# Attention and gated feed-forward on one core: own tiles for the copied sums, fewer exponential tiles, weight splits queued later

## The chip, the cores and the metric

One core of a Trainium2 chip runs the whole kernel in one launch. The metric is the device time of an execution in microseconds; three runs were taken, and the median is used. A profile of one further execution goes with them.

## What is computed

Input `x` has 2048 tokens of 512 features. All data are float32.

```
xn = layernorm(x)
q, k, v = split(xn @ wqkv)             # 32 heads of 16 features
s = concat_heads(softmax(q k^T / 4) v) @ wo
g = silu(((xn @ w_gate) * (xn @ w_up)) @ w_down)      # 1792 hidden features
out = x + s * g
```

## The kernel before

**Precision.** Products of weights and activations are made of three products of a fast float32 format: a value is split into a high part (a cast) and a low part (value minus high part), and high by high, high by low and low by high are added up. Weights are loaded in float32 into a "raw" tile and split by GpSimd, two instructions a tile: `split`, `split_raw`, `split_rows`. Scores carry the split in their contraction (48 rows: high, high, low against high, low, high), and the product of probabilities and V is in plain float32.

**Attention.** Heads go in 8 groups of 4, queries in 4 chunks of 512, so there are 32 units (`NU`), each of 16 rounds (`kt`, 128 keys each). In a round the main loop does, for each of the 4 heads `j`:
- `expo`: a matmul `t` of keys by queries into a PSUM bank of the pool `st` (3 banks), then the exponential by ScalarE into a tile `e` from `etile()`;
- `score`: a matmul `s` of queries by keys for the unit ahead (`LEAD` = 21 rounds ahead), and VectorE's maximum over it. Two more rows of the `t` matmul subtract that maximum;
- `step()`, which runs work that was put off by `soon(n, fn)` for n steps, and at some `j` (`GAPS`) a piece of filler.

At every even round `values()` runs the work in `before_values`, steps the finishing of heads, and calls `block(prev)`: 8 matmuls of the 8 `e` tiles of the two rounds before by V, in four column groups, into another bank of `st` named `pv`. ScalarE copies that bank. A unit's first block is copied into the tile `acc` (1 buffer); each later one goes into another `etile()`, and GpSimd adds it to `acc`. `etile()` has `EBUFS` = 12 buffers, shared by the exponentials, the copied sums and, at the start, raw weights of V.

**Heads.** `finish(i)` is a generator that `values()` steps: transpose `acc` into `tr` (VectorE), reciprocal of the row sums, multiply the heads into a tile `on` (GpSimd, or VectorE for the last four units), transpose `on` back into `tr`, and store it to DRAM (`OD`). For the last unit the heads stay on the chip and are split by `last_heads`.

**Filler.** The projections, the feed-forward part (`ffn`) and the output projection (`ending`) are generators whose matmuls are dealt out between the score matmuls by `Filler`, 6 gaps a cycle of two rounds, and a row of sums (`pair`) over two or three cycles. `pair` uses the lower and the upper 64 rows of TensorE at once. After its first half ScalarE reads one element (`look`), after its second `ffn` copies `g` on ScalarE, and VectorE multiplies `u` by `g` at the next `values()`. A row's last matmuls fall on gap 2 of an even round, so that the copy stands in ScalarE's program between the third and the fourth exponential of that round.

**Order.** The instructions of TensorE, ScalarE and VectorE keep the order in which the program gives them. GpSimd and the DMA queue of SyncE are put in order when the program is built, by a scheduler that takes what is ready by its own reckoning; only for the first 18 rounds is their order tied too. A tile that is used again waits for the last use of what was in it.

Of the kernel before, what the change touches and what calls it, by code (L numbers as in the profile page):

```python
# [11 lines left out]
F32 = mybir.dt.float32  # L12
# [7 lines left out]
P = 128  # L20
# [13 lines left out]
GAPS = [(0, 1, 2), (1, 2, 3)]  # L34
SLOTS = 24 * (NC * (NG // 2 - 1) + 1) + 36 * NF * NC
SPLIT_ROUNDS = 4
EBUFS = 12
HBUFS = 2
QBUFS = 2
FINAL_AT = 8  # L40
# [9 lines left out]
def body(ctx, tc, x, wqkv, wo, wg, wu, wd, out):  # L50
# [53 lines left out]
        pool.memset(V[:, tts, H * VW:], 1.0)  # L104

    ones_columns(slice(0, 8))
    on = keep.tile([P, 16, 32], F32, name="on")
    pool.memset(on, 0.0)

    fst = {}  # L110

# [36 lines left out]
    def etile():  # L148
        return ep.tile([P, 512], F32, name="e", bufs=EBUFS)

    qkv = ExitStack()
    qp = qkv.enter_context(tc.tile_pool(name="qkv", bufs=1))
    xh, xl = [[(qp if c else keep).tile([P, ND, 512], F32R, name=f"{n}{c}" if c else f"f{n[1]}") for c in range(NC)]
# [5 lines left out]
    def split(name, src):  # L159

        raw = wtile(name + "r")
        dma(raw, src.rearrange("(d p) f -> p d f", p=P))
        return split_raw(name, raw)

    def split_raw(name, raw, after=None):
        hi, lo = [wtile(name + n) for n in "hl"]
        cast = pool.tensor_copy(hi, raw)
        if after is not None:
            tc.add_manual_dep(cast.ins, after.ins.name, BEHIND, reason="keeps the port free for the layer norm")
        pool.tensor_tensor(lo, raw, hi, op=OP.subtract)  # L170
        return hi, lo
# [184 lines left out]
    def gu_weights(f):  # L356
        fs = slice(f * P, (f + 1) * P)
        return [split(n, w[:, fs]) for n, w in (("w1", wg), ("w0", wu))]

    def ffn(nxt):  # L360
        fp = fst["fp"]
        for c in range(NC):
            if c == 0:
                fh, fl = xh[0], xl[0]
            else:
                fh, fl = [keep.tile([P, ND, 512], F32R, name=n) for n in ("fh", "fl")]
                dmar(fh, XD[c][0])
                dmar(fl, XD[c][1])
            y = fp.tile([P, 4, D], F32, name="y")
            for ti, fs in enumerate(THIRDS):  # L370
                hh = fp.tile([P, 5, 512], F32R, name="hh")
                hl = fp.tile([P, 5, 512], F32R, name="hl")
                dh = fp.tile([P, 5, D], F32R, name="dh")
                dl = fp.tile([P, 5, D], F32R, name="dl")
                for i, f in enumerate(fs):
                    ws = nxt
                    if not (c == NC - 1 and f == NF - 1):
                        nxt = gu_weights((f + 1) % NF)
                    outs = []
                    yield from pair(outs, [("misc", f"{n}{c}_{f}") for n in "gu"], [terms(lambda d: wh[:, d], lambda d: wl[:, d],  # L380
                                                 lambda d: fh[:, d], lambda d: fl[:, d], ND) for wh, wl in ws])
                    g = fp.tile([P, 512], F32, name="g", bufs=1)
                    nc.scalar.activation(g, outs[0], AF.Copy)
                    h = fp.tile([P, 512], F32, name="h", bufs=1)
                    before_values.append(lambda h=h, u=outs[1], g=g, hi=hh[:, i], lo=hl[:, i]: product(h, u, g, hi, lo))
                    raw = fp.tile([P, D], F32, name="wdr", bufs=2)
                    dma(raw, wd[f * P:(f + 1) * P])
                    pool.tensor_copy(dh[:, i], raw)
                    pool.tensor_tensor(dl[:, i], raw, dh[:, i], op=OP.subtract)
                if c == NC - 1 and fs[-1] == NF - 1:  # L390
                    fst["y"] = y
                    fst["w"] = [keep.tile([P, ND, D], F32R, name=n) for n in ("fh", "fl")]
                    for d in range(ND):
                        raw = fp.tile([P, D], F32, name="wdr", bufs=2)
                        dma(raw, wo[d * P:(d + 1) * P])
                        split_rows(raw, *[t[:, d] for t in fst["w"]])
                for t in range(0, 4, 2):
                    outs = []
                    yield from pair(outs, [("misc", f"y{c}_{ti}_{u}") for u in (t, t + 1)], [terms(lambda i: hh[:, i, u * P:(u + 1) * P],
                                                 lambda i: hl[:, i, u * P:(u + 1) * P],  # L400
                                                 lambda i: dh[:, i], lambda i: dl[:, i], len(fs)) for u in (t, t + 1)])
                    for n, o in enumerate(outs):
                        def add(o=o, y=y[:, t + n], first=ti == 0, n=n):
                            if first and n:
                                nc.vector.tensor_copy(y, o)
                            elif first:
                                nc.scalar.activation(y, o, AF.Copy)
                            else:
                                nc.vector.tensor_tensor(y, o, y, op=OP.add)
                        before_values.append(add)  # L410
            later.append(silu(fp, c, y))
# [205 lines left out]
    def block(todo):  # L617

        i = todo[0][0]
        g = i // NC  # L620
        o = psum("st", f"pv{i}")
        for n, (_, kt, es) in enumerate(todo):
            for j in range(4):
                h0 = (4 * g + j) * VW
                nc.tensor.matmul(o[32 * j:32 * j + 32], V[:, kt, h0:h0 + 32], es[j],  # L625
                                 start=n == 0, stop=n == len(todo) - 1)
        if todo[0][1] == 0:
            sums[i] = keep.tile([P, 512], F32, name="acc", bufs=1)
            nc.scalar.activation(sums[i], o, AF.Copy)
        elif i == NU - 1 and kt >= NT - 2:  # L630
            nc.vector.tensor_tensor(sums[i], o, sums[i], op=OP.add)
        else:
            part = etile()
            nc.scalar.activation(part, o, AF.Copy)  # L634
            pool.tensor_tensor(sums[i], sums[i], part, op=OP.add)

    def finish(i):

        g, c = divmod(i, NC)
        tr = keep.tile([P, 16, 32], F32, name="tr", bufs=1)  # L640
        tn = tr.rearrange("p b e -> p (b e)")
        yield
        nc.vector.transpose(tn, sums.pop(i))
        rc = keep.tile([P, 16, 1], F32, name="rc", bufs=1)
        nc.vector.reciprocal(rc, tr[:, :, DH:DH + 1])
        late = i >= NU - NC
        (nc.vector if late else pool).tensor_tensor(on[:, :, 0:DH], tr[:, :, 0:DH], rc.to_broadcast([P, 16, DH]),
                                                         op=OP.mult)
        yield
        nc.vector.transpose(tn, on.rearrange("p b e -> p (b e)"))  # L650
        if i == NU - 1:
            fst["tn"] = tn
            return
        dma(OD[c][4 * g:4 * g + 4], tn)
        finished.add(i)


# [6 lines left out]
    def early():  # L664
# [5 lines left out]
        for which in (1, 0):  # L670
            wraw.append(wtile(f"w{which}r"))
            dma(wraw[-1], wqkv[:, which * D:which * D + P].rearrange("(d p) f -> p d f", p=P))
        norm["raws"] = raws = [etile() for _ in range(ND)]
        for d in range(ND):
            dma(raws[d], wqkv[d * P:(d + 1) * P, 2 * D:])
        for tt in range(4, NT):
# [7 lines left out]

        def warm(n):
            for _ in range(n):
                nc.tensor.matmul(psum("x", "warm"), ident, on.rearrange("p b e -> p (b e)"), start=True, stop=True)

        warm(6)
        first = (0, 1), (2, 3)  # L690
# [76 lines left out]
    def filler(wq0):  # L767
        yield from proj_pair(0, [(wq0, 0, 2), (wq0, 0, 3)])
        for m in range(1, NG // 2):
            wk, wq = fst.get(("qk", m)) or (qk_weights(m, 1), qk_weights(m, 0))  # L770
            for c in range(NC):
                yield from proj_pair(m, [(wk, 1, c), (wq, 0, c)])
                if m == 1 and c:
                    after = fst["high"].ins.name
                    for n, src in enumerate((xh, xl)):
                        put = sync.dma_start(XD[c][n].bitcast(F32), src[c].bitcast(F32))
                        tc.add_manual_dep(put.ins, after, BEHIND, reason="not before the first exponentials")
                if m == NG // 2 - 1 and c == NC - 2:
                    nxt = gu_weights(0)
        run_ahead()  # L780
        flush()
        qkv.close()
        fst["fp"] = ffp.enter_context(tc.tile_pool(name="ffn", bufs=1, reuse_waits="tile"))
        yield from ffn(nxt)
# [52 lines left out]
    prev = []  # L837

    def values():
        run_ahead()  # L840
        step_small(heads)
        block(prev)
        if prev[-1][1] == NT - 1:
            heads.append(finish(prev[0][0]))
            step_small(heads)
        prev.clear()
# [63 lines left out]
```

## Time and profile before

| | |
|---|---|
| median of 3 runs | 1803.99 us (1798.45 to 1805.04) |
| profiled execution | 1804.02 us, its span 1802.2 us |
| TensorE (PE) busy | 1758.0 us, 98% |
| VectorE (DVE) busy | 1447.8 us, 80% |
| ScalarE (ACT) busy | 1326.7 us, 74% |
| GpSimd (POOL) busy | 891.8 us, 49% |
| granted TensorE clock | 0.988 |

A row of the timeline reads: start and duration in us, engine, line, operation, tiles written and read, shape, count, and in brackets the engine's idle time before it and what ended it. A row of the waits reads: who waited, for whom, us in total, times, the longest. PEld is TensorE's loading of weights, which runs beside its matmuls. A matmul's end is modelled, so TensorE is read by the starts of its matmuls.

### The profile page before, as it was taken

What the parts mean: (1) busy time and instruction counts of PE and PEld (TensorE: products, weight loads), DVE (VectorE), ACT (ScalarE), POOL (GpSimd) and SP (SyncE); (2) the same over time, 40 slices, a digit from 0 to 9 for tenths busy, and PEclk for the clock granted to TensorE, in tenths of its full rate; (3) what the DMA queues carried; (4) which work ended last, traced back from release to release, by engine and by line L of the source; (5) the groups of instructions that cost most, each with busy time, mean ns of one, the idle gap of its engine ahead of it and who ended that gap; (6) DMA issues with size and microseconds to landing.
All of it is one profiled execution on the core that took longest, in us unless ns stands there. A gap on an engine that the chain in (4) does not pass through costs nothing.

```text
span 1802.2 us, 35104 instructions
## 1 busy us (share of the span) xinstructions
PE 1758.0 (98%) x13578; PEld 1064.8 (59%) x13578; DVE 1447.8 (80%) x2440; ACT 1326.7 (74%) x2576; POOL 891.8 (49%) x920
## 2 busy tenths in 40 slices
PE   9999999899999999999999999999999999998897
PEld 5656556565665666566556665566655566555544
DVE  6878888788888888888888888888878888887613
ACT  5357777677777778777777877777777777776663
POOL 4314554653644556365354755435466365355641
PEclk9999999999999999999999999999999999999989
DMA  5317524511231312321132211312233121111421
GB/s 199 115 57 229 199 99 127 141 41 44 63 69 52 97 50 66 71 69 48 38 84 84 80 49 57 75 40 63 80 77 82 29 68 51 40 46 47 157 86 70
DMA packets 117234, 145.78 MB, mean 81 GB/s; under 512 B 12620, under 2 KB 74060, under 8 KB 114380
## 3 DMA queue, kind: packets, MB, share of 16 engines
q1 hardware_dynamic: 117068, 143.55, 27.1%
q8 instruction: 106, 1.74, 0.4%
q14 instruction: 60, 0.49, 0.1%
HBM read 95.94 MB, written 47.45 MB: 80 GB/s over the span
## 4 chain that ended last, share of the span: by engine, by line
PE 86%; POOL 6%; DMA 2%; issue 2%; DVE 2%; ACT 2%; SPq 0%; POOLq 0%; ACTq 0%; DVEq 0%
PE pv L625 23%; PE t L612 17%; PE s L587 12%; PE g L275 5%; PE y L275 5%; PE g L279 4%; PE u L275 4%; PE y L279 4%; PE u L279 3%; PE p L275 2%; PE v L256 2%; PE p L279 1%; PE z L275 1%; POOL acc L64 1%; DVE mx L589 1%
## 5 line engine op out<-in xcount | busy, mean ns | idle before, releaser
L589 DVE TENSOR_REDUCE mx<-s 128x1 f32<-128x512 f32 x2048 | 1278.1, 684 | 260.1 <-PE s L587 181.4
L614 ACT ACTIVATE e<-t 128x512 f32<-128x512 f32 x2048 | 1117.7, 605 | 125.5 <-POOL acc L64 52.9
L612 PE MATMUL t<-qs,ks 50*128 50x512 f32 x2048 | 811.1, 417 | 28.0 <-ACT e L614 25.4
L587 PE MATMUL s<-ks,qs 48*128 48x512 f32 x2048 | 802.8, 422 | 2.6 <-DVE mx L589 2.5
L612 PEld LDWEIGHTS t<-qs,ks 50*128 50x128 f32 x2048 | 363.7, 187 | 330.3 <-ACT e L614 131.1
L64 POOL TENSOR_TENSOR acc<-acc,e 128x512 f32<-128x512 f32 x223 | 290.8, 1304 | 484.3 <-ACT e L634 481.7
L625 PE MATMUL pv<-e,V 128*32 128x512 f32 x4096 | 494.3, 600 | 0.0
L587 PEld LDWEIGHTS s<-ks,qs 48*128 48x128 f32 x2048 | 353.1, 186 | 35.4 <-DVE mx L589 6.4
L634 ACT ACTIVATE e<-pv 128x512 f32<-128x512 f32 x223 | 133.3, 598 | 229.8 <-PE pv L625 229.6
L625 PEld LDWEIGHTS pv<-e,V 128*32 128x32 f32 x4096 | 107.3, 109 | 239.7 <-issue 188.3
L64 POOL CAST w0h<-w0r 128x512 fp32r<-128x512 f32 x60 | 36.6, 611 | 135.5 <-PE u L275 64.0
L279 PE MATMUL g<-fh,w1h 64*128 64x512 f32 x224 | 91.0, 406 | 0.0
L279 PE MATMUL y<-dh,hh 64*128 64x512 f32 x224 | 90.3, 403 | 0.0
L275 PE MATMUL u<-fh,w0h 64*128 64x512 f32 x224 | 89.5, 400 | 0.0
L279 PE MATMUL u<-fh,w0h 64*128 64x512 f32 x224 | 89.0, 397 | 0.0
L275 PE MATMUL y<-dh,hh 64*128 64x512 f32 x224 | 88.8, 396 | 0.0
L279 PE MATMUL u<-fh,w0l 64*128 64x512 f32 x224 | 88.7, 396 | 0.0
L275 PE MATMUL y<-dl,hh 64*128 64x512 f32 x224 | 88.6, 396 | 0.0
L275 PE MATMUL g<-fh,w1h 64*128 64x512 f32 x224 | 88.5, 395 | 0.0
L275 PE MATMUL g<-fh,w1l 64*128 64x512 f32 x224 | 88.5, 395 | 0.0
L275 PE MATMUL u<-fl,w0h 64*128 64x512 f32 x224 | 88.4, 395 | 0.0
L279 PE MATMUL u<-fl,w0h 64*128 64x512 f32 x224 | 88.4, 395 | 0.0
(257 smaller groups left out, 3061.9 us busy)
## 6 DMA issues: line engine op xcount, KB each, us to landing
w1r<-in_wg_dram SPq DMA_DIRECT2D x56, 256.0 KB
w0r<-in_wu_dram SPq DMA_DIRECT2D x56, 256.0 KB
wdr<-in_wd_dram SPq DMA_DIRECT2D x56, 256.0 KB
qs<-QD SPq DMA_DIRECT2D x64, 192.0 KB
ks<-KD SPq DMA_DIRECT2D x12, 768.0 KB
KD<-hl SPq DMA_DIRECT2D x16, 512.0 KB
QD<-hl SPq DMA_DIRECT2D x16, 512.0 KB
OD<-tr SPq DMA_DIRECT2D x31, 256.0 KB
```

The source lines that it names most:

```text
L64: got = getattr(self.engine, name)(*args, **kw)
L256: nc.tensor.matmul(o, l(d), r(d), start=k == d == 0, stop=k == 2 and d == ND - 1)
L275: nc.tensor.matmul(outs[k], l[LOWER], r[LOWER], start=k == 0 and n == 0, stop=(stop or k == 0) and n == len(low) - 1, skip_group_check=k == 1)
L279: nc.tensor.matmul(outs[1 - k], l[UPPER], r[UPPER], start=k == 0 and m == 0, stop=(stop or k == 0) and m == len(high) - 1, skip_group_chec ...
L587: nc.tensor.matmul(o, QS[i][b:b + KB, pr, t * P:(t + 1) * P], k[b:b + KB, pr, kc * 512:(kc + 1) * 512], start=True, stop=True)
L589: nc.vector.tensor_reduce(MX[i][:, j, t, kc:kc + 1], o, axis=AX.X, op=OP.max)
L612: nc.tensor.matmul(o, k[b:b + KR, pr, kt * P:(kt + 1) * P], QS[i][b:b + KR, pr], start=True, stop=True)
L614: nc.scalar.activation(e, o, AF.Exp, scale=DH ** -0.5)
L625: nc.tensor.matmul(o[32 * j:32 * j + 32], V[:, kt, h0:h0 + 32], es[j], start=n == 0, stop=n == len(todo) - 1)
L634: nc.scalar.activation(part, o, AF.Copy)
```

## The change

- `EBUFS` goes from 12 to 10. The copied sums of blocks get two tiles of their own (`parts()`, `PBUFS` = 2), and so do two of the raw weights at the start.
- `acc` has 2 buffers. The zeroed tile `on` is gone; the warming matmuls at the start read a zeroed `acc` instead.
- `finish` multiplies the heads in place in `tr` and transposes them back into the unit's `acc`, which is stored. For the last two units it runs at once, without pauses, and VectorE adds the last block of unit 30 as it did for unit 31.
- `values()` steps the heads only where `before_values` is empty.
- `split` puts its two GpSimd instructions off by 6 steps. The load of `w_down` moves ahead of the pair `g`, `u`, and its split is put off by 8 steps. The projections' weights for the next group are asked for at chunk 2 of the group before.

```diff
-EBUFS = 12
+EBUFS = 10
+PBUFS = 2
...
-    on = keep.tile([P, 16, 32], F32, name="on")
-    pool.memset(on, 0.0)
+    idle = keep.tile([P, 512], F32, name="acc", bufs=2)
+    pool.memset(idle, 0.0)
...
+    def parts():
+        return ep.tile([P, 512], F32, name="part", bufs=PBUFS)
...
         raw = wtile(name + "r")
         dma(raw, src.rearrange("(d p) f -> p d f", p=P))
-        return split_raw(name, raw)
+        hl = [wtile(name + n) for n in "hl"]
+        soon(6, lambda: split_rows(raw, *hl))
+        return hl
...
                         nxt = gu_weights((f + 1) % NF)
+                    raw = fp.tile([P, D], F32, name="wdr", bufs=2)
+                    dma(raw, wd[f * P:(f + 1) * P])
+                    soon(8, lambda raw=raw, i=i, dh=dh, dl=dl: split_rows(raw, dh[:, i], dl[:, i]))
                     outs = []
...
-                    raw = fp.tile([P, D], F32, name="wdr", bufs=2)
-                    dma(raw, wd[f * P:(f + 1) * P])
-                    pool.tensor_copy(dh[:, i], raw)
-                    pool.tensor_tensor(dl[:, i], raw, dh[:, i], op=OP.subtract)
...
         if todo[0][1] == 0:
-            sums[i] = keep.tile([P, 512], F32, name="acc", bufs=1)
+            sums[i] = keep.tile([P, 512], F32, name="acc", bufs=2)
             nc.scalar.activation(sums[i], o, AF.Copy)
-        elif i == NU - 1 and kt >= NT - 2:
+        elif i >= NU - 2 and kt >= NT - 2:
             nc.vector.tensor_tensor(sums[i], o, sums[i], op=OP.add)
         else:
-            part = etile()
+            part = parts()
             nc.scalar.activation(part, o, AF.Copy)
             pool.tensor_tensor(sums[i], sums[i], part, op=OP.add)
...
         tr = keep.tile([P, 16, 32], F32, name="tr", bufs=1)
-        tn = tr.rearrange("p b e -> p (b e)")
-        yield
-        nc.vector.transpose(tn, sums.pop(i))
+        acc = sums.pop(i)
+        late = i >= NU - 2
+        if not late:
+            yield
+        nc.vector.transpose(tr.rearrange("p b e -> p (b e)"), acc)
         rc = keep.tile([P, 16, 1], F32, name="rc", bufs=1)
         nc.vector.reciprocal(rc, tr[:, :, DH:DH + 1])
-        late = i >= NU - NC
-        (nc.vector if late else pool).tensor_tensor(on[:, :, 0:DH], tr[:, :, 0:DH], rc.to_broadcast([P, 16, DH]),
-                                                         op=OP.mult)
-        yield
-        nc.vector.transpose(tn, on.rearrange("p b e -> p (b e)"))
+        (nc.vector if i >= NU - NC else pool).tensor_tensor(tr[:, :, 0:DH], tr[:, :, 0:DH],
+                                                            rc.to_broadcast([P, 16, DH]), op=OP.mult)
+        if not late:
+            yield
+        nc.vector.transpose(acc, tr.rearrange("p b e -> p (b e)"))
         if i == NU - 1:
-            fst["tn"] = tn
+            fst["tn"] = acc
             return
-        dma(OD[c][4 * g:4 * g + 4], tn)
+        dma(OD[c][4 * g:4 * g + 4], acc)
         finished.add(i)
...
-            wk, wq = fst.get(("qk", m)) or (qk_weights(m, 1), qk_weights(m, 0))
+            wk, wq = fst["qk", m]
             for c in range(NC):
+                if c == 2 and m + 1 < NG // 2:
+                    fst["qk", m + 1] = qk_weights(m + 1, 1), qk_weights(m + 1, 0)
                 yield from proj_pair(m, [(wk, 1, c), (wq, 0, c)])
...
     def values():
-        run_ahead()
-        step_small(heads)
+        if before_values:
+            run_ahead()
+        else:
+            step_small(heads)
         block(prev)
```

More of the change, by code (lines that the diff above doesn't have):

```diff
@@ L672, in early @@
             dma(wraw[-1], wqkv[:, which * D:which * D + P].rearrange("(d p) f -> p d f", p=P))
-        norm["raws"] = raws = [etile() for _ in range(ND)]
+        norm["raws"] = raws = [etile() if d < 2 else parts() for d in range(ND)]
         for d in range(ND):
@@ L686, in warm @@
             for _ in range(n):
-                nc.tensor.matmul(psum("x", "warm"), ident, on.rearrange("p b e -> p (b e)"), start=True, stop=True)
+                nc.tensor.matmul(psum("x", "warm"), ident, idle, start=True, stop=True)
         warm(6)
```

## The prediction

> **What bounds the kernel now.** I read the page's busy times first, then the timeline of ordinary rounds, the waits, and the timeline again where a wait is long.
>
> ```profile
> PE 1758.0 (98%) x13578; PEld 1064.8 (59%) x13578; DVE 1447.8 (80%) x2440; ACT 1326.7 (74%) x2576; POOL 891.8 (49%) x920
> ```
>
> TensorE is busy in 98% of the span; nothing else is near. So a change pays only by what it takes from, or adds to, TensorE's standing time. The attention loop gives TensorE one block of probability-times-V matmuls (L625) per two rounds. I call the time from one block's start to the next's a cycle, and count within it from the block's start, P. There are 256. One with a full load of filler (24 matmuls), after a `g` copy, and the start of the next:
>
> ```profile
> 1004.74 0.60 ACT L383 ACTIVATE g<-g 128x512 f32<-128x512 f32 x1
> 1004.87 1.92 PE L625 MATMUL pv<-e,V 128*32 128x512 f32 x16
> 1005.22 0.61 ACT L614 ACTIVATE e<-t 128x512 f32<-128x512 f32 x1
> 1006.72 0.50 PE L612 MATMUL t<-qs,ks 50*128 50x512 f32 x1
> 1006.86 0.60 ACT L634 ACTIVATE e<-pv 128x512 f32<-128x512 f32 x1 [0.52 <-PE pv L625]
> 1007.07 0.39 PE L612 MATMUL t<-qs,ks 50*128 50x512 f32 x1
> 1007.29 0.39 PE L275 MATMUL g<-fh,w1h 64*128 64x512 f32 x1
> 1007.75 0.39 PE L612 MATMUL t<-qs,ks 50*128 50x512 f32 x1
> 1011.60 1.93 PE L625 MATMUL pv<-e,V 128*32 128x512 f32 x16
> ```
>
> The cycle lasts 6.73 us. In it: the block to P+1.92; the first score matmul `t` at P+1.85, the second at P+2.20, the first filler at P+2.42, the third `t` at P+2.88. The third waits for the copy of the block's sums (P+1.99 to 2.59), since `st` has three PSUM banks. The second needs the bank that the fourth exponential of the round before the block empties. That one starts at P+0.35 and ends at P+0.96, with 1.2 us to spare. That spare time is what the change spends.
>
> Where is TensorE kept standing now? The waits:
>
> ```profile
> ACT e L614 <- POOL acc L64: 52.9, 36, 6.7
> PE t L612 <- ACT e L614: 25.4, 13, 5.0
> ACT acc L629 <- DVE tr L643: 9.2, 9, 2.1
> ```
>
> 36 times the fourth exponential waits for GpSimd's addition of the block before, because its `e` buffer was the one that held the block's copied sums. 13 times it is so late that TensorE itself stands. The first of these, the two largest, and between them a middling one with the next block's start:
>
> ```profile
> 192.30 0.50 PE L612 MATMUL t<-qs,ks 50*128 50x512 f32 x1 [0.58 <-ACT e L614]
> 331.51 1.92 PE L625 MATMUL pv<-e,V 128*32 128x512 f32 x16
> 337.31 0.60 ACT L614 ACTIVATE e<-t 128x512 f32<-128x512 f32 x1 [5.22 <-POOL acc L64]
> 337.96 0.79 PE L612 MATMUL t<-qs,ks 50*128 50x512 f32 x1 [4.10 <-ACT e L614]
> 344.83 1.92 PE L625 MATMUL pv<-e,V 128*32 128x512 f32 x16
> 347.19 0.60 ACT L614 ACTIVATE e<-t 128x512 f32<-128x512 f32 x1 [2.34 <-PE s L587]
> 347.84 0.49 PE L612 MATMUL t<-qs,ks 50*128 50x512 f32 x1 [0.67 <-ACT e L614]
> 348.18 0.40 PE L275 MATMUL u<-fh,w0h 64*128 64x512 f32 x1
> 352.48 1.92 PE L625 MATMUL pv<-e,V 128*32 128x512 f32 x16
> 1637.32 1.92 PE L625 MATMUL pv<-e,V 128*32 128x512 f32 x16
> 1644.70 0.79 PE L612 MATMUL t<-qs,ks 50*128 50x512 f32 x1 [5.03 <-ACT e L614]
> ```
>
> The middling one is my scale. The exponential ends at P+2.96, the second `t` issues 0.05 later, and the filler comes 0.34 behind it, not 0.22: a matmul that meets an idle TensorE costs 0.12 more. Late by 0.81 + 0.12 = 0.93; the cycle lasts 7.65 instead of 6.73, 0.92 longer. What is lost there comes back nowhere.
>
> **Part 1: ten `e` tiles instead of twelve (a loss).** A block reads the eight tiles of the two rounds before while the current round fills its own four: twelve. With ten, the third and fourth exponentials need the tiles that the block's first two matmuls read. In the built order they wait for those two, which now signal for themselves; before, only the block's last one did. When do they end?
>
> ```profile
> 1011.60 0.16 PEld L625 LDWEIGHTS pv<-e,V 128*32 128x32 f32 x8 [0.37 <-ACT e L614]
> 1012.06 0.13 PEld L625 LDWEIGHTS pv<-e,V 128*32 128x32 f32 x4 [0.30 <-issue]
> L625 PE MATMUL pv<-e,V 128*32 128x512 f32 x4096 | 494.3, 600 | 0.0
> ```
>
> The program's 8 matmuls run as 16, each in two halves, four at a time over four column groups. The later loads at P+0.46 mark the second four starting. If these are the second halves of the first four tiles, a tile is free at 0.46 + 0.60 = P+1.06; with the 0.07 that the copy shows behind the block's end, ScalarE starts at P+1.13. If both halves were among the first four, it would be P+0.69. One column group cannot take two halves at once, so I take 1.13. No later bound is open: each of the two signals by itself.
>
> The third exponential then runs from P+1.13. ScalarE takes its next work 0.48 later (1004.74 to 1005.22). The fourth runs from P+1.61 to 2.21, and the second `t` goes at P+2.26: 0.06 late, plus 0.12 for an idle TensorE: 0.18. But a `g` copy, or its like in the projections, stands in ScalarE's order between the two. Then the fourth runs from P+2.09 to 2.69, and `t` goes at 2.74: 0.54 + 0.12 = 0.66 late. How often?
>
> ```profile
> L383 ACT ACTIVATE g<-g 128x512 f32<-128x512 f32 x56 | 34.1, 609 | 0.0
> L312 ACT ACTIVATE qr<-p 128x512 f32<-128x512 f32 x13 | 8.0, 612 | 0.0
> L589 DVE TENSOR_REDUCE mx<-s 128x1 f32<-128x512 f32 x2048 | 1278.1, 684 | 260.1 <-PE s L587 181.4
> ```
>
> 69 cycles, each the first of its filler pair and full: 69 x 0.66 = 46 us. Of the other 174 up to 1691 us, 85 carry 18 or more filler matmuls and lose 0.18 to 0.23 (the tiny `look` read adds 0.05): 17 us. In 89, with 16 or fewer, the eight reductions of 684 ns pace TensorE, and 0.18 fits beside them: 0 to 2 us. Some 20 cycles have one more ScalarE copy behind the fourth exponential; it pushes the sums' copy past the third `t`, about 0.35 each: 7 us. Loss: 70 us, 17 by the earlier release (69 x 0.22, plus 2).
>
> **Part 2: own tiles for the copied sums (a gain).** Now the copy, not the exponential, waits for GpSimd, and for the addition two blocks back: about 12 us may pass instead of 5. The additions stand in GpSimd's built order where they stood, and the bursts of w_down splits are as long; I count nothing for the later queueing. The two largest stalls (13.32 - 6.73 = 6.6 us at 331.5; 7.6 at 1637.3) had additions late by less than that, and go. With a third of 4.0 and seven of 0.75 to 1.0 (the first is the `t` at 192.30 above, the last in the cycle at 1630): 24 us. Next in line is GpSimd's order for the hidden-layer splits, whose readers are a pair or more away.
>
> **Part 3: two tiles for a unit's sums, heads in place.** The copy that waited for the transpose no longer does. Six cycles were 0.46 to 0.77 longer by it: 3.4 us. Stepping the heads only where no other VectorE work is due takes perhaps half of 2.4 us of crowded cycles: 1. The in-place product and the transposes are as many and as large: 0.
>
> **Part 4: the end.** The heads of unit 30 finish four rounds sooner, so the output projection's third chunk moves into two cycles that had no filler, and its two pairs leave the tail.
>
> ```profile
> 1691.28 1.93 PE L625 MATMUL pv<-e,V 128*32 128x512 f32 x16
> 1742.50 1.92 PE L625 MATMUL pv<-e,V 128*32 128x512 f32 x16
> 1748.14 1.92 PE L625 MATMUL pv<-e,V 128*32 128x512 f32 x16
> 1768.17 1.93 PE L625 MATMUL pv<-e,V 128*32 128x512 f32 x16
> 1774.06 1.92 PE L625 MATMUL pv<-e,V 128*32 128x512 f32 x16
> 1778.09 1.93 PE L625 MATMUL pv<-e,V 128*32 128x512 f32 x16
> 1783.73 0.69 DVE L544 TENSOR_TENSOR h<-tr,g 128x512 fp32r<-128x512 f32 x1 [0.69 <-ACT g L543]
> 1796.62 0.40 PE L523 MATMUL z<-hl,h 128*128 128x512 f32 x1
> 1797.87 0.69 DVE L450 TENSOR_TENSOR y<-z,hh 128x512 f32<-128x512 f32 x1
> ```
>
> The twelve cycles from 1691.28 to 1778.09 take 86.8 us; three stand on late additions. In their place: one of 6.8, ten of 6.0 (1768.17 to 1774.06 is 5.89, plus 0.1 from part 1), one of 4.1: 70.9. I add 4 us: unit 31's row maxima still queue behind twelve GpSimd instructions, and VectorE's next output rows behind them, which held nothing up while TensorE stood anyway. 12 us gained. Then the last heads: their low halves are ready at 1784.42, and only the twelve last matmuls (0.23 each) and VectorE's six steps of 0.7 remain, to about 1789.6 instead of 1798.56: 9 us. Together 21.
>
> **Sum.** The profiled execution took 1804.02 us (1802.2 of span, 1.8 around it); the median, 1803.99, is the same. 1804 + 70 - 24 - 4 - 21 = 1825; I say 1824.
>
> Two rules of the Trainium skill bear on this. In the trace, every `t` and `s` matmul signals and the next follows at 0.22 to 0.23 us, so a signal costs nothing visible. "TensorE: Matmul & The Clock Gate", The cost: per-tile semaphore tail, puts 26.3 ns on each increment; by it the two new ones per block would add an estimated 255 x 2 x 26 = 13 us, hence 1837. And a gap now about to recur in every cycle is what "Perfetto Trace Analysis", Identifying Performance Opportunities, calls consistent bubbles, which it says can mean too few buffers for the next tile; it agrees with part 1.
>
> **The rivals.** *Faster, the early release.* The first four matmuls free the tiles at P+0.69; the price of part 1 is 17, the gains stay: 1804 + 17 - 49 = 1772. It decides if the third exponential starts before P+0.8. For it: nothing in the rows names the halves. Against: the column groups. 0.12. *About the same, a milder loss.* Neither the idle cost nor the small delays count, only 69 x 0.54 and the 7: 44 us, so 1804 + 44 - 49 = 1799. For it: exponentials ending at P+1.9 delay nothing now, and no row lies between there and P+2.7. 0.16. *Much slower, stalls that stay.* The bursts still hold the additions beyond two blocks, or TensorE outruns the weight splits; parts 2 and 3 give nothing: 1804 + 70 - 21 = 1853. 0.07. *The increments* lengthen the block by 0.05: 1837. 0.05. The forecast: 0.60.
>
> **How the numbers follow.** About 0.5%, 9 us, is what a measurement of this kernel can tell from no change: 1795 to 1813. The forecast's own range, 1806 to 1842, takes part 1 between 55 and 85 and the gains between 43 and 55; a tenth of it lies below 1813. To leave out no more than two in ten I reach down across the milder loss to 1780, where the early release's own range begins, and up to 1845. Faster: the early release and a third of the milder loss: 0.17. Same: the rest of that and the forecast's low end: 0.17. Slower: 0.66.
>
> **What would show it.** Right: the third exponential of every even round starts near P+1.1; after a `g` the second `t` goes near P+2.7, and a full cycle lasts 7.4 instead of 6.73, others 6.9; ScalarE no longer waits for `acc` additions in its exponentials; no stall of several us at the places of 331, 1330 and 1637; filler in every cycle near the end, and some 15 us from the last full block to the end. Wrong: full cycles of 6.73 throughout, which makes it a faster kernel; or copies of sums waiting for GpSimd for microseconds, which is the slow rival.

## The result and the profile after

The changed kernel takes 1833.38 us (median; 1830.96 to 1833.97) against 1804.1 for the kernel before (1798.45 to 1805.04): 1.0166 times as long, with an interval of 1.0144 to 1.0189. The forecast was 1824, slower. The profiled execution took 1833.15 us, 1831.4 of it span.

From the page of the changed kernel, the busy times; then four rows of its waits (who waited for whom, us in total, times, the longest). TensorE counts 26.9 us more of busy time with as many matmuls, so its share of the span, 97% against 98%, does not show the loss; the waits and the starts of blocks do. The mean granted clock was 0.995, against 0.988 before.

```profile
PE 1784.9 (97%) x13578; PEld 1074.6 (59%) x13578; DVE 1479.7 (81%) x2441; ACT 1297.9 (71%) x2575; POOL 884.3 (48%) x919
```

```profile
ACT e L619 <- PE pv L630: 410.8, 255, 1.9
PEld t L617 <- ACT e L619: 282.6, 610, 0.8
...
DVE h L349 <- ACT g L392: 62.1, 55, 1.5
...
PE t L617 <- ACT e L619: 24.6, 69, 0.4
```

In every cycle (255 times) an exponential now waits for the block's matmuls; before, no exponential did. TensorE waits for an exponential 69 times, 0.4 us at most: those are the 69 cycles with a `g` or `qr` copy, and no longer 13 times up to 5.0. The additions by GpSimd have gone from the list of what an exponential waits for. VectorE has a new wait as well: its product `h` needs the `g` copy, which is late too, 62.1 us in all; that stands beside TensorE's work.

One full cycle with a `g` copy, and the start of the next, which has a `look`, in the timeline of the changed kernel:

```profile
1068.02 1.93 PE L630 MATMUL pv<-e,V 128*32 128x512 f32 x16
...
1069.10 0.60 ACT L619 ACTIVATE e<-t 128x512 f32<-128x512 f32 x1 [1.24 <-PE pv L630]
1069.59 0.59 ACT L392 ACTIVATE g<-g 128x512 f32<-128x512 f32 x1
...
1069.87 0.49 PE L617 MATMUL t<-qs,ks 50*128 50x512 f32 x1
...
1070.07 0.60 ACT L619 ACTIVATE e<-t 128x512 f32<-128x512 f32 x1
...
1070.55 0.62 ACT L639 ACTIVATE part<-pv 128x512 f32<-128x512 f32 x1
...
1070.73 0.49 PE L617 MATMUL t<-qs,ks 50*128 50x512 f32 x1 [0.35 <-ACT e L619]
...
1071.53 0.39 PE L617 MATMUL t<-qs,ks 50*128 50x512 f32 x1
...
1075.44 1.92 PE L630 MATMUL pv<-e,V 128*32 128x512 f32 x16
...
1076.53 0.60 ACT L619 ACTIVATE e<-t 128x512 f32<-128x512 f32 x1 [1.79 <-PE pv L630]
...
1077.02 0.14 ACT L289 ACTIVATE look<-u 1x1 f32<-1x1 f32 x1
1077.07 0.57 ACT L619 ACTIVATE e<-t 128x512 f32<-128x512 f32 x1
...
1077.70 0.50 PE L617 MATMUL t<-qs,ks 50*128 50x512 f32 x1
```

From the block's start P = 1068.02: the third exponential at P+1.08, the copy `g` at P+1.57, the fourth exponential at P+2.05, the second `t` at P+2.71 instead of P+2.20. The cycle lasts 7.42 us instead of 6.73. In the next one only the tiny `look` stands between, the second `t` goes at P+2.26, and that cycle lasts 6.9. Nothing that came late is caught up.

The old stalls at 331, 1330 and 1637 are gone. Two new ones have come. The first is early in the feed-forward part (timeline, then two windows: stretch, length, busy time and count of PE, PEld, DVE, ACT and POOL, granted clock, DMA share, GB/s):

```profile
353.15 1.92 PE L630 MATMUL pv<-e,V 128*32 128x512 f32 x16
...
357.72 0.69 DVE L349 TENSOR_TENSOR h<-u,g 128x512 f32<-128x512 f32 x1 [3.37 <-POOL hl L65]
...
358.46 0.59 PE L285 MATMUL u<-fh,w0h 64*128 64x512 f32 x1 [1.80 <-DVE h L349]
...
363.71 1.93 PE L630 MATMUL pv<-e,V 128*32 128x512 f32 x16
```

```profile
355.50:358.40 2.90, 0.81 (x4) 0.37 (x3) 0.68 (x2) 1.89 (x4) 2.90 (x3) 1.00 0.35 99
358.40:362.20 3.80, 3.74 (x18) 2.96 (x20) 2.59 (x5) 1.29 (x3) 3.80 (x5) 0.55 0.02 4
```

`h` has one buffer. VectorE cannot write the next one before GpSimd has split the last, and GpSimd is busy without a break over these windows. Behind `h` on VectorE stand the row maxima, which free the banks of `s`. The cycle lasts 10.56 instead of 6.02. Part of that is the clock: after the pause it was 0.55 for 3.8 us. That the one buffer of `h` makes this stall is read from the chain of waits; no run gave `h` a second buffer. With the tiles alone the same cycle lasts 8.31 (run `tiles_alone` below), and why it is longer here stays open.

The second is in the output projection, in the timeline:

```profile
1749.51 1.93 PE L630 MATMUL pv<-e,V 128*32 128x512 f32 x16
...
1751.02 0.21 DVE L605 STREAM_TRANSPOSE mt<-mm 128x32 f32<-128x32 f32 x1 [6.78 <-POOL mm L65]
1751.16 0.67 DVE L458 TENSOR_TENSOR hh<-z,hh 128x512 f32<-128x512 f32 x1
...
1751.54 1.26 POOL L65 TENSOR_TENSOR acc<-acc,part 128x512 f32<-128x512 f32 x1
...
1751.86 3.94 DVE L459 TENSOR_TENSOR hh<-hh 128x512 f32<-128x512 f32 x1
...
1752.77 1.25 POOL L65 TENSOR_TENSOR y<-e,y 128x512 f32<-128x512 f32 x1
1753.99 1.25 POOL L65 TENSOR_TENSOR acc<-acc,part 128x512 f32<-128x512 f32 x1
...
1756.43 0.69 DVE L459 TENSOR_TENSOR hh<-hh 128x512 f32<-128x512 f32 x1
...
1756.45 0.79 PE L285 MATMUL z<-fh,hl 64*128 64x512 f32 x1 [4.08 <-DVE hh L458]
...
1762.47 1.92 PE L630 MATMUL pv<-e,V 128*32 128x512 f32 x16
```

VectorE stands 6.78 us before the transpose of unit 31's row maxima, which GpSimd gives it late; then one output row takes 3.94 us where the same step took 0.69 a little later. Only then is the bank of `z` free, and the cycle lasts 12.96.

**The account.** I take each cycle up to the 244th block, less the length that an undisturbed cycle with as many filler matmuls had before (6.73 with 24, 6.47 with 22, 6.02 with 18, 5.98 to 6.21 with fewer), and sum by what stands in ScalarE's order. For the end I take the starts of blocks and the end of the span.

| step of the prediction | predicted | in the two traces |
|---|---|---|
| part 1, 69 cycles after `g` or `qr` | +46 | +47 |
| part 1, all others and the extra copies | +24 | +22 |
| parts 2 and 3, stalls and waits that go | -28 | -31 |
| new stalls before the end (353: 4.5; 1692: 1.7; 166: 1.35) | 0 | +7.5 |
| part 4, the last twelve cycles (79.75 against 86.8) | -12 | -7 |
| part 4, from the last block to the end (15.4 against 24.2) | -9 | -8.7 |
| the loop begins earlier | 0 | -0.7 |
| sum | +21 | +29 |

The spans differ by 1831.4 - 1802.2 = 29.2.

### The profile page after: what moved, and what is told of

It is laid out like the page before. It is cut to its first block, busy times and chain, and to the rows that moved or that the text cites. A ratio compares the mean times of both kernels' runs of the same rounds, so it can differ in the third digit from the quotient of the medians.

```text
span 1831.4 us, 35270 instructions
## 1 busy us (share of the span) xinstructions
PE 1784.9 (97%) x13578; PEld 1074.6 (59%) x13578; DVE 1479.7 (81%) x2441; ACT 1297.9 (71%) x2575; POOL 884.3 (48%) x919
## 4 chain that ended last, share of the span: by engine, by line
PE 88%; ACT 5%; issue 3%; POOL 2%; DMA 1%; DVE 1%; SPq 0%; ACTq 0%; POOLq 0%; DVEq 0%
PE pv L630 22%; PE t L617 20%; PE s L592 10%; PE g L285 5%; PE u L285 5%; PE y L281 4%; PE y L285 4%; PE g L281 4%; PE u L281 3%; ACT e L619 2%; PE p L285 2%; PE v L262 2%; PE p L281 2%; ACT g L392 1%; PE z L285 1%
## 5 line engine op out<-in xcount | busy, mean ns | idle before, releaser
L594 DVE TENSOR_REDUCE mx<-s 128x1 f32<-128x512 f32 x2048 | 1305.1, 685 | 209.3 <-PE s L592 163.2
L617 PE MATMUL t<-qs,ks 50*128 50x512 f32 x2048 | 846.9, 425 | 25.6 <-ACT e L619 24.6
L592 PE MATMUL s<-ks,qs 48*128 48x512 f32 x2048 | 835.1, 428 | 3.3 <-DVE mx L594 2.5
L617 PEld LDWEIGHTS t<-qs,ks 50*128 50x128 f32 x2048 | 377.9, 185 | 370.3 <-ACT e L619 282.6
L65 POOL TENSOR_TENSOR acc<-acc,part 128x512 f32<-128x512 f32 x222 | 286.4, 1290 | 465.4 <-ACT part L639 465.3
L592 PEld LDWEIGHTS s<-ks,qs 48*128 48x128 f32 x2048 | 368.8, 184 | 31.2 <-issue 6.1
L639 ACT ACTIVATE part<-pv 128x512 f32<-128x512 f32 x222 | 134.2, 604 | 0.8 <-POOL acc L65 0.7
L349 DVE TENSOR_TENSOR h<-u,g 128x512 f32<-128x512 f32 x56 | 38.7, 692 | 65.4 <-ACT g L392 62.1
L285 PE MATMUL u<-fl,w0h 64*128 64x512 f32 x224 | 88.5, 395 | 0.0
L281 PE MATMUL g<-fl,w1h 64*128 64x512 f32 x224 | 88.2, 394 | 0.0
```

What stands on the lines that cost most here:

```text
L65: got = getattr(self.engine, name)(*args, **kw)
L281: nc.tensor.matmul(outs[k], l[LOWER], r[LOWER], start=k == 0 and n == 0, stop=(stop or k == 0) and n == len(low) - 1, skip_group_check=k == 1)
L285: nc.tensor.matmul(outs[1 - k], l[UPPER], r[UPPER], start=k == 0 and m == 0, stop=(stop or k == 0) and m == len(high) - 1, skip_group_chec ...
L349: nc.vector.tensor_tensor(h, u, g, op=OP.mult)
L592: nc.tensor.matmul(o, QS[i][b:b + KB, pr, t * P:(t + 1) * P], k[b:b + KB, pr, kc * 512:(kc + 1) * 512], start=True, stop=True)
L594: nc.vector.tensor_reduce(MX[i][:, j, t, kc:kc + 1], o, axis=AX.X, op=OP.max)
```

## The experiments

The kernel before took 1802.4 to 1803.0 beside these runs.

**The tiles put back.** `EBUFS` = 12 and the sums in `e` tiles; all else as changed.

```diff
-EBUFS = 10
-PBUFS = 2
+EBUFS = 12
...
-            part = parts()
+            part = etile()
...
```

> The changed kernel with its tiles put back: twelve `e` tiles, from which the copied sums take theirs again; two `acc` tiles, heads in place, later weight splits and the end as changed. Theory (the exponentials that wait for the block cost about 68 us, the own tiles give about 24 back): the third and fourth exponentials start before the block's end again, full cycles of 6.73, stalls of several us near 331, 1330 and 1637 come back: 1804 - 4 - 16 = 1784, within 6. Rival (the later weight splits and the head steps slow the loop): 1825 to 1835, with cycles as long as in the changed kernel.

Measured: 1786.78 (1785.17 to 1789.17), 0.9915 of before (0.99 to 0.993). Its waits:

```profile
ACT e L615 <- POOL acc L64: 54.6, 36, 6.5
...
PE t L613 <- ACT e L615: 22.4, 13, 5.0
```

The 36 waits for GpSimd and TensorE's 13 are back, nearly as many us as before, though not all at the same places (the cycle at 189 lasts 13.3 instead of 7.0, the one at 1637 before 11.0 instead of 13.6). Full cycles last 6.73. So what is left of the change without its tiles is a gain of 16, and the whole loss lies in the tiles.

**The tiles alone**, on the kernel before.

```diff
-EBUFS = 12
+EBUFS = 10
+PBUFS = 2
...
-            part = etile()
+            part = parts()
...
```

> The kernel before with ten `e` tiles and two own tiles for the copied sums, and nothing else of the change. Theory: 1804 + 68 - 24 = 1848, with full cycles of 7.4 after a `g` or `qr` copy and 6.9 without. Rival (the loop is slowed by the rest of the change): 1800 to 1812, since the own tiles then only gain.

Measured: 1855.78 (1854.64 to 1856.98), 1.0299 (1.0282 to 1.0316). Its waits:

```profile
PE t L616 <- ACT e L618: 24.6, 69, 0.4
...
ACT acc L633 <- DVE tr L647: 11.1, 10, 3.8
...
PE t L616 <- ACT acc L633: 8.6, 11, 3.6
```

The 69 waits are the same. It is 8 us more than expected, and most of that shows in the last row: with ten tiles the copies run late, and the copy of a new unit's sums, with a single `acc`, now holds TensorE 11 times, 8.6 us in all; in the kernel before it was 6 times and 1.8 us. Several such cycles with a `g` copy last 0.8 longer than their like (8.25 against 7.4). So the second `acc`, worth 3.4 us by itself in the prediction, is worth more beside ten `e` tiles; the edits don't add up singly.

**The copy first.** The third exponential of an even round is issued behind the filler's copy.

```diff
+                hold = [] if n and n % 2 == 0 and j == 2 else None
-                es.append(expo(i, kt, j))
+                es.append(expo(i, kt, j, hold))
...
                     fil.part(n % 2 and j == 1)
+                if hold:
+                    hold.pop()()
...
```

> The changed kernel with the third exponential of each even round handed to ScalarE behind the `g` or `qr` copy instead of ahead of it; tensor work and tiles as in the changed kernel. Theory (the copy, standing in ScalarE's order between two exponentials that wait, makes 0.5 of each 0.66): the copy runs before P+0.5, the third exponential at P+1.1, the fourth at P+1.6 to 2.2, those cycles last 6.9 instead of 7.4; 69 x 0.5 = 35 us less, 1798. Rival (the loss is the two more signals of the block, or the wait of the third exponential by itself): 1830 to 1835.

Measured: 1794.49 (1793.63 to 1795.13), 0.9956 (0.9942 to 0.9971). A full cycle with a `g` copy and the next start, in its timeline:

```profile
1056.52 0.60 ACT L392 ACTIVATE g<-g 128x512 f32<-128x512 f32 x1 [0.61 <-PE u L281]
...
1056.62 1.92 PE L633 MATMUL pv<-e,V 128*32 128x512 f32 x16
...
1057.70 0.60 ACT L622 ACTIVATE e<-t 128x512 f32<-128x512 f32 x1 [0.58 <-PE pv L633]
1058.19 0.59 ACT L620 ACTIVATE e<-t 128x512 f32<-128x512 f32 x1
...
1058.84 0.50 PE L617 MATMUL t<-qs,ks 50*128 50x512 f32 x1
...
1063.48 1.93 PE L633 MATMUL pv<-e,V 128*32 128x512 f32 x16
```

The copy runs before the block, the exponentials at P+1.08 and P+1.57, the second `t` at P+2.22, and the cycle lasts 6.86 instead of 7.42. Of the 39 us gained, the 69 cycles with a copy hold 38; 3 of these are a shorter stall at 346 (the one at 353 before), so some 35 us come from the order of three instructions on ScalarE. The kernel is then faster than before by a little.

**One more `e` tile, one own tile fewer**, in the same memory.

```diff
-EBUFS = 10
-PBUFS = 2
+EBUFS = 11
+PBUFS = 1
...
```

> The changed kernel with eleven `e` tiles and one own tile for the copied sums, in the same memory. Theory: only the fourth exponential waits for the block (P+1.08 to 1.68), the copy runs ahead of it, the second `t` goes at P+2.20 and the loss of 68 is gone; the copy of the sums waits for GpSimd's addition of one block back, which leaves about 13 us of the old stalls: 1833 - 68 + 13 = 1778, between 1765 and 1785. Rival (one wait for the block costs half of two): 1800 to 1812.

Measured: 1782.51 (1780.39 to 1784.49), 0.989 (0.9875 to 0.9905). A full cycle with a `g` copy and the next start, in its timeline:

```profile
1040.31 0.65 ACT L392 ACTIVATE g<-g 128x512 f32<-128x512 f32 x1
...
1040.35 1.93 PE L630 MATMUL pv<-e,V 128*32 128x512 f32 x16
...
1041.43 0.60 ACT L619 ACTIVATE e<-t 128x512 f32<-128x512 f32 x1 [0.47 <-PE pv L630]
...
1042.54 0.39 PE L617 MATMUL t<-qs,ks 50*128 50x512 f32 x1
...
1047.06 1.93 PE L630 MATMUL pv<-e,V 128*32 128x512 f32 x16
```

An exponential still waits for the block in every cycle, at the same P+1.08. But it is the fourth and no copy stands ahead of it; it ends at P+1.68, the second `t` goes at P+2.19, and the cycle lasts 6.71. One wait for the block costs nothing and two cost 69 us, 47 of it in the 69 cycles with the copy between them. The price of the single own tile shows in this kernel's waits:

```profile
ACT part L639 <- POOL acc L65: 21.5, 7, 5.8
```

**The splits queued at once.** `split` and the split of `w_down` without `soon`, the load and split of `w_down` behind the pair as before; the projections' weights are still asked for at chunk 2.

```diff
-        hl = [wtile(name + n) for n in "hl"]
-        soon(6, lambda: split_rows(raw, *hl))
-        return hl
+        return split_raw(name, raw)
...
-                    soon(8, lambda raw=raw, i=i, dh=dh, dl=dl: split_rows(raw, dh[:, i], dl[:, i]))
...
+                    split_rows(raw, dh[:, i], dl[:, i])
```

> The changed kernel with its weight splits queued on GpSimd at once, as before, instead of six or eight steps later. Theory (the place of the splits in GpSimd's order moves only single stalls): the stall at 353 us shrinks from 4.5 to about 2.3, as in the kernel with the tiles alone, the rest stays: 1828 to 1834. Rival (the later splits carry a share of the 68 us): 1800 to 1820.

Measured: 1840.98 (1838.54 to 1841.76), 1.0214 (1.0199 to 1.0229). Neither expectation: the stall at 353 (361 here) is 4.5 us as before, and a new one comes, in its timeline:

```profile
174.16 0.71 DVE L648 STREAM_TRANSPOSE tr<-acc 128x512 f32<-128x512 f32 x1 [7.05 <-POOL acc L65]
...
175.76 0.79 PE L590 MATMUL s<-ks,qs 48*128 48x512 f32 x1 [5.55 <-DVE mx L592]
```

The additions of a unit's last sums stand behind weight splits, VectorE's transpose waits for them, and the row maxima wait behind the transpose: that cycle lasts 13.8, where the changed kernel has 7.3. So the delay is worth about 6.5 us at one place and costs nothing elsewhere; it is no part of the loss. It only makes up for something else in the change: the kernel before and the one with the tiles alone queue their splits at once too, and this cycle lasts 5.98 in both.

**The end alone**, on the kernel before: the last two units' heads at once, VectorE adding unit 30's last sums.

```diff
-        elif i == NU - 1 and kt >= NT - 2:
+        elif i >= NU - 2 and kt >= NT - 2:
...
-        yield
+        if i < NU - 2:
+            yield
```

> The kernel before with the late heads of the last two units finished at once and VectorE adding the last sums of unit 30, and nothing else of the change. Theory: the gain that the changed kernel's end shows by itself, 16: 1788. The prediction's term, 21: 1783. Rival (the gain needs the other edits, since a late addition still holds unit 30): 1800 to 1806.

Measured: 1787.78 (1784.72 to 1790.3), 0.992 (0.9904 to 0.9936). From the 244th block to the end it takes 95.1 us, the changed kernel 95.2, the kernel before 111.0. The gain stands by itself, and it is 16. That it equals the changed kernel's within 0.1 us is chance, for it is made up otherwise: here the two cycles that stood on late additions and began at 1691 and 1701 before are still there (9.33 and 12.66 us, against 9.49 and 12.36), while the others last about 5.9; in the changed kernel those two are gone (6.84 and 6.48), but one of 12.96 has come, and most others last 6.1 to 6.5.

**The late output rows through PSUM.**

```diff
-        if t % 2 and c == NC - 1:
+        late = now[0] >= NU * 16 - LEAD and c < NC - 1
+        if late or t % 2 and c == NC - 1:
             nc.vector.tensor_tensor(o, o, yt, op=OP.mult)
             nc.vector.tensor_tensor(yt, o, xt, op=OP.add)
...
```

> The changed kernel with the product of the output projection's late rows left in PSUM, so that VectorE's second step reads PSUM and one SBUF operand instead of two SBUF operands. Theory (VectorE's step with all operands in SBUF is held up while GpSimd runs an operation of its own on SBUF: 3.94 us at 1751.86 instead of 0.69): no such step over 0.75 us, and the stall at 1749 loses about 3 us: 1829. Rival (only the wait for the row maxima makes this stall, and the 3.94 us cover another wait): 1833, and a step as long as before.

Measured: 1831.94 (1827.36 to 1834.29), 1.0157 (1.0137 to 1.0178). The second step's group (count, then busy us and mean ns), first in the changed kernel, then here:

```profile
L459 DVE TENSOR_TENSOR hh<-hh 128x512 f32<-128x512 f32 x4 | 6.0, 1505 | 0.1
```

```profile
L456 DVE TENSOR_TENSOR hh<-z,hh 128x512 f32<-128x512 f32 x4 | 2.8, 692 | 0.1
```

One of these four in the timeline, and the GpSimd operation that ran the whole time beside it:

```profile
1756.43 1.26 POOL L65 TENSOR_TENSOR y<-e,y 128x512 f32<-128x512 f32 x1
...
1756.84 0.69 DVE L456 TENSOR_TENSOR hh<-z,hh 128x512 f32<-128x512 f32 x1
```

The long step is gone and the cycle of 12.96 at 1749 lasts 9.95, as the first theory said. The median does not show it: in this profile the stall at 1692 was 1.8 longer and the one at 353 0.5, and the interval overlaps that of the changed kernel. The mechanism is shown, a gain in time is not.

**Eleven tiles, and the second own tile from the feed-forward part's memory.** I wanted both gains at once: eleven `e` tiles and one own tile, and from the feed-forward part on a second one, `part2`, in memory that the projections leave; output rows as above.

```diff
     def parts():
+        turn[0] += 1
+        if "fp" in fst and turn[0] % 2:
+            return fst["fp"].tile([P, 512], F32, name="part2", bufs=1)
...
```

> The changed kernel with eleven `e` tiles throughout, one own tile for copied sums until the feed-forward part and a second one from that part's memory after it; late output rows through PSUM. Theory: no loss of part 1, the old stalls gone after 330 us, one stall of 5.6 near 190 us as with eleven tiles and one own tile, the stall at 353 as in the changed kernel: 1833 - 68 + 6 - 3 = 1768. Rival (stalls of GpSimd's queue grow once TensorE runs ahead): 1778 to 1785.

Measured: 1777.61 (1776.08 to 1777.99), 0.9863 (0.9848 to 0.9878), at the rival's end, but for another reason. In its timeline:

```profile
325.97 0.60 ACT L644 ACTIVATE part<-pv 128x512 f32<-128x512 f32 x1 [8.03 <-DMA QD<-hl]
```

The first copy into `part2` waits for the store of the tile that had lain there: a stall of 9.2 us, once. So the second tile is taken later (the difference to the last run):

```diff
-        if "fp" in fst and turn[0] % 2:
+        if now[0] >= 68 and turn[0] % 2:
```

> As eleven_two, but the second own tile is taken from round 68 on, some four rounds after the memory of the projections is handed over, so that the copy of the sums does not wait for the store of `hl` from the same place. Theory (that wait made the 9.2 us stall at 316): the stall goes, one of up to 4.5 may come at 350 as in the changed kernel: 1778 - 9 + 0 to 4 = 1768 to 1773. Rival (GpSimd's queue at this place holds TensorE in any case): 1776 to 1779.

Measured: 1769.23 (1766.11 to 1770.82), 0.9814 (0.98 to 0.9827). The stall is gone; at 348 a small one of 1.4 is left, at 190 one of 5.1, and near the end two cycles last 10.94 (at 1632) and 10.55 (at 1689).

Then, on top of that, the row maxima of the last two units are transposed 12 steps after their reduction:

```diff
-                maxima(si, 8 if si < NU - 1 else 4)
+                maxima(si, 8 if si < NU - 2 else 12)
```

> As eleven_later, and the row maxima of the last two units are transposed on VectorE 12 steps after their reduction instead of 8 and 4. Theory (VectorE's sums and output rows stand behind a transpose that waits for GpSimd): the stalls of 4.0 and 4.1 at 1640 and 1697 fall to under 2 each: 4 us less than eleven_later. Rival (the maxima then come too late for the scores of these units): a new wait of the first `t` of unit 30 or 31, and no gain.

Measured: 1768.57 (1765.85 to 1769.13), 0.9809 (0.9796 to 0.9822): no different from the last. Those two cycles are down to 6.95 and 6.65, but in their place, in a cycle of 11.05, stands what the rival named, in the timeline:

```profile
1699.06 0.76 PE L622 MATMUL t<-qs,ks 50*128 50x512 f32 x1 [3.15 <-DMA qs<-MD]
```

This is the first `t` of unit 31, whose maxima now reach `qs` too late. Either kernel is faster than both that were to be compared, by 34 us against the one before.

## Why the prediction was right, and by how much its steps were off

**Part 1** was right in mechanism, place and size. The block's first signal of a free tile lands at P+1.06, as forecast, and the third exponential starts 0.02 behind it, at P+1.08 (1.13 forecast); the second `t` after a copy goes at P+2.71 (2.74) and without one at P+2.22 to 2.26 (2.26). Most full cycles last 7.33 to 7.43 with a copy and 6.85 to 6.95 without. 69 us measured against 70. The 69 cycles were not all full, as the prediction had them: 31 carry 18 filler matmuls, but most of these lose about as much (6.64 to 6.74 instead of 6.02). In the other 174 two errors cancel: the 85 with 18 or more and the extra copies lost 16 us, the 89 with fewer 6; forecast were 24 and 0 to 2. One more tile takes the loss away, ten tiles alone bring it, and the copy's place in ScalarE's order makes about half of it: all three by runs. That the 0.12 of an idle TensorE counts also where the second `t` is only 0.02 to 0.06 late (a plain full cycle is 0.12 to 0.15 longer) is what told the forecast from the milder loss of 44.

**Parts 2 and 3**: 28 forecast, 31 found. The stalls did go. But "next in line is GpSimd's order for the hidden-layer splits, whose readers are a pair or more away" was wrong: the tile `h`, which those splits read, has one buffer, and its next writer, VectorE, stands right behind. At 353 that cost 4.5 us, and two smaller stalls, of the same kind (VectorE's queue behind something late from GpSimd), 3 more. Of the 4.5 at 353, the tiles alone bring 2.3; the delay of the splits does not bring the rest (4.5 with it and without it). The later splits, counted at nothing, kept a stall of 6.5 away near 166, which neither the kernel before nor the tiles alone have.

**Part 4**: 21 forecast, 16 found, and 16 also when the end is changed by itself. The tail's 9 was right; the twelve cycles gained 7 instead of 12. The 4 us allowed for unit 31's row maxima became 7 (12.96 in the cycle at 1749 instead of 6.0), and 2 more lie in the others, of which most last 6.1 to 6.5 instead of 6.0. The place and the cause of the 7 were the ones named, GpSimd's queue ahead of the maxima and VectorE's rows behind them, though not by the count named: six GpSimd instructions, not twelve, end between 1744.24, when VectorE has reduced the maxima, and 1750.77, when GpSimd takes them up. What was not seen is that VectorE's second step for a row, with both operands in SBUF, then also had to wait out GpSimd: about 3 us of it, by the run through PSUM.

**The rivals.** The early release fell with P+1.08. *The increments*: the block gives three signals instead of one, yet the first `t` goes at P+1.85 in both kernels (1004.87 to 1006.72 before, 1068.02 to 1069.87 after), and the block's last signal lands at P+1.97 in both. The 26.3 ns that the Trainium skill, "TensorE: Matmul & The Clock Gate", The cost: per-tile semaphore tail, puts on each increment do not show here. The stalls that stay did not happen as put: copies of sums waited 0.7 us in all for GpSimd. The 9 us that the forecast fell short are mainly two mis-sized terms, 7.5 for new stalls (put at nothing) and 5 at the end, less 3 for more stalls gone; that the last offsets some of the others is luck.

## What to carry to other kernels

When buffers are taken away, count which instruction then waits for which matmul, and what stands ahead of it in its engine's order: here one wait for the running block cost nothing, and the second, often with a copy of 0.6 us between the two, cost 69 us. Where that can't be avoided, the copy goes ahead of the waiting instruction. Curing a stall uncovers the next buffer in the same queue, so look at every single-buffered tile that the late engine reads.

## What the runs showed of the hardware that was not expected

- VectorE's addition of two SBUF operands took 3.94 us while GpSimd ran three SBUF operations of 1.25 back to back (1751.54 to 1755.24); the three others of its kind in this trace ran beside no GpSimd operation and took 0.69. With one operand in PSUM the step took 0.69 also beside a GpSimd operation (1756.84 in the run through PSUM). The Trainium skill, "SBUF — State Buffer", Who interferes with whom, says that a VectorE instruction with two SBUF inputs contends with a GpSimd instruction that reads SBUF, and calls the port pair that the two engines share "an exclusive lock". The trace agrees, and shows the VectorE instruction held over more than one of GpSimd's.
- After 2.9 us in which TensorE was busy for 0.81 (355.5 to 358.4), the granted clock was 0.55 for 3.8 us. Behind the wait of 4.08 that ended at 1756.45 it was 0.50 for 3.8 us (1756.4 to 1760.2). A stall of this length is paid for again behind it.
- The first matmul of a block, of the 16 that the trace counts for 8, frees its tile only about 1.05 us after the block's start, more than half of the 1.92 that the block takes. The waiting exponential starts at P+1.08 in every kernel here with ten or eleven `e` tiles. The trace of the changed kernel shows why, and settles what the prediction could only choose: the two early signals are those of the fifth and the sixth of the 16 matmuls, which start at P+0.45 and end at about P+1.05, and they land at P+1.06 and P+1.10.
